# Block sums of the first token group asked for later in a fused window-attention and mixture-of-experts kernel, with its order of issue refitted

## The chip, the cores and the metric

The kernel runs on one core of a Trainium2 chip. The metric is the device time of one launch in microseconds; each version is run several times and the median counts. One more execution is taken with the hardware profiler; every statement about single instructions comes from that one. Five engines run side by side, each with its own queue in program order: PE (matrix products and weight loads), DVE (vector), ACT (scalar: exponentials, copies), POOL (GpSimd) and SP (issue of transfers).

## What is computed

Two layers follow each other. The first is attention over 4 batches, 8 heads, 768 positions and head size 64, in which each position sees the 4 first positions (the sinks) and the last 128. The second is a mixture of 4 experts over the 3072 tokens that come out, each of width 512, with all experts added up under normalised weights:

```python
scores = scale * np.matmul(q, k.transpose(0, 1, 3, 2))
keep = is_sink | in_window
a = np.exp(scores - max); a = a / a.sum(-1)
x = np.matmul(a, v)                  # laid out as (3072, 512)
p = domain_probs / (domain_probs.sum(-1, keepdims=True) + 1e-09)
for e in range(4):
    h = np.maximum(x @ w1[e], 0.0)   # w1[e]: 512 x 1024
    out += p[:, e:e + 1] * (h @ w2[e])
```

## The kernel before

**Tiles and stages.** Each batch of 768 tokens is cut into three groups of 256 tokens, named (batch, group). Attention for a group goes, for each pair of heads, through scores (PE, L704), exponentials (ACT, tile `aT`, L744), a mask (DVE, L752 in batch 0, L725 later), products with the values (PE, tile `od`, L777 and L784), division by the row sum (reciprocal `R` L811 on DVE, then L814 on DVE in batch 0 or L823 on ACT later; result `onat`), and a transposition into `xT`. In batch 0 PE transposes (tile `tx`, L845) and ACT or DVE copies to `xT` (L300); in later batches a transposing DMA does it (L801). Sink scores are separate products (PE, L665), and their exponentials are `sinkA` (ACT, L673). The transposed queries and keys are `qkT`; in batch 0 PE transposes them too (L593, L596) and ACT or DVE copies (L300).

**Experts.** The first layer of an expert is done in one of two ways. The plain way (L1098, tile `hps`) takes eight products of 256 columns per quarter. The fast way is Strassen's scheme: seven half-size products P1, P5, P6, P2, P7, P3, P4 (PE, L1181, tile `cps`) instead of eight. Its moving operands are blocks of `xT` or four sums and differences of them, the **block sums** `T`, formed on DVE by four subtractions (L1150); its weights are blocks of w1 or sums of them (`vf`, or `qkn` for two experts, L402 to L408). Between the products ACT copies partial results (L1224, L1237, L1199), DVE adds (L1231 makes the operand that P7 waits for, L1246 the one that P4 waits for) and applies ReLU and gate (L1215). When a bank of PSUM holds old partial marks, one extra product of 512 columns, the **seed**, clears it (L1189). The second layer is plain for two groups (L1425, tile `acc`, gathered by DVE at L1435 and L1437 into `osb`), and Strassen's scheme for the others (L1350, with sums `S` made on DVE at L1275 and L1296, weight sums `wf` at L367 to L373, results gathered at L1379 to L1397).

**Which units are fast.** `START` says from which (batch, group) on an expert is fast: expert 0 from (1,0), expert 1 from (0,1), experts 2 and 3 from (0,0). So (0,0) needs block sums for experts 2 and 3 and (0,1) for experts 1, 2 and 3.

**What sets the order.** The program is straight-line code; its order is written by a planner that runs while the kernel is built. The planner keeps a clock per engine (`t["pe"]`, `t["dve"]`, ...) from fitted costs. The loop at L1486 lists what PE could do next, each choice with a time from which it is ready and a priority (`LOW_PRODUCT`, `LOW_SECOND`, `EARLY`, `OPEN`, `STEP0` and others, lower first), emits one, and advances the clock. Work for DVE, ACT and POOL is put on a list with a due time (ready time plus a slack such as `GATE`, `GATE0`, `FORM`, `TOKEN0`, `MARGIN`); `flush` (L165) emits it by due time when the planner's clock of that engine reaches it. Work marked "any" goes to ACT or DVE, whichever is free first by that clock: the copies of `tx` and `tr` are such. On the chip each engine then keeps this order and waits on semaphores. The planner's clock is not the chip's.

**Around the change.** `tokens()` (L1130) asks for block sums, one group after another in the order of the groups; at most `NT3` = 3 sets live at a time. A group is asked for when its `xT` is complete by the planner's clock:

```python
at = max(xT_at.get((b, hp, g), 1e12) for hp in range(NHP))
if at > t["pe"]:
    return
```

The four subtractions are then put on DVE's list one after another, each with slack `TOKEN0` in batch 0 (L1149 to L1156). The second reads the result of the first and the fourth that of the second.

Of the kernel before, what the change touches and what calls it, by code (L numbers as in the profile page):

```python
# [16 lines left out]
def kernel(  # L17
# [47 lines left out]
    SHARE_OF = (0.635, 1.148, 0.943)  # L65
    LEAD = (1.227, 0.235)
    DUE = 0
    LOW_PRODUCT = 2.816
    LOW_SECOND = 4.296
    HIGH_PRODUCT = 0.403  # L70
    EARLY = 0.138
    GATE = 5742
    GATE0 = 5043
    FORM = 19230
    FORM2 = 38137
    TOKEN0 = 220
    WAIT2 = 19401
    WAIT1 = 6201
    LATE3 = 3
    TOKEN = 11696  # L80
    MARGIN = 828
    FULL = 8
    STEP0 = 0.155
    READY = 39
    WIDE = 2
    OPEN = 1.336
    ONACT = 1
    ONE = 2
    PAIR = 1
# [16 lines left out]
    t = {"pe": 1200.0, "act": 0.0, "dve": 0.0, "pool": 1280.0, "sp": 800.0, "sw": 6500.0, "hw": 0.0}  # L106
    ring, whole = [0.0] * 6, [False] * 6
    WARM = 6600.0
    FLIP = 179
    LATE = 2342  # L110
    LATE1 = 12449

    def pe(cols, *deps, n=1, switch=0):
# [12 lines left out]
    def dve(cols, *deps, rate=0.96, fixed=157, shared=None):  # L126
        at = max([t["dve"], *deps])
        if rate == 1.92 if shared is None else shared:
            at += max(0.0, port["pool"] - at - 78)
            port["dve"] = at + fixed + cols / rate  # L130
        t["dve"] = at + fixed - 85 + cols / rate
        return at + fixed + 35 + cols / rate
# [10 lines left out]
    def free_at(n=1):  # L143

        return sorted(ring)[n - 1]
# [15 lines left out]
    def later(engine, ready, slack, run):  # L161

        pend.append((ready, ready + slack, engine, run))
# [48 lines left out]
    def sp(*deps, issue=530, takes=600, turning=False):  # L212
        t["sp"] = max([t["sp"], *deps]) + issue
        at = max(t["hw"], t["sp"] + 800)
        row = next((x[3] for x in moved if x[1] <= at < x[2]), 0.0)
        if turning and row:
            t["hw"] = at + TURNED * (row + SHARE)
            t["sw"] += TURNED * SHARE
            for x in moved:
                if x[2] > at:  # L220
                    x[1] += TURNED * SHARE * (x[1] > at)
                    x[2] += TURNED * SHARE
                    landed[x[0]] = x[2] + 900
                    if x[0][0] == "w1" and ("w1", x[0][1]) in landed:
                        landed["w1", x[0][1]] = max(landed["w1", x[0][1]], x[2] + 900)
        else:
            t["hw"] = at + takes + max(0.0, min(takes, t["sw"] - at)) * (not turning)
        return t["hw"] + 900
# [46 lines left out]
    def turn_nat(b, tb):  # L275
# [6 lines left out]
        )  # L282
        turned_at[b, tb] = sp(landed["qk", b, tb], scored_at.get(b - 1, 0.0), issue=1330, takes=1400, turning=True) + (LATE1 if b == 1 else LATE)

# [144 lines left out]
    def next_form():  # L429
# [11 lines left out]
        forming.append(x)  # L441
        later("dve", t["pe"], FORM if x[0] is weight_form1 else FORM2, run)
        return True
# [417 lines left out]
    class Attention:  # L861
# [29 lines left out]
        def options(self):  # L891
# [16 lines left out]
            if self.flips:  # L908
                yield self.flip_ready() + (FLIP if self.b == 0 and self.flips[0][2] else 0), "flip"

# [54 lines left out]
    class Mixture:  # L965
# [77 lines left out]
        def firsts(self):  # L1043
# [4 lines left out]
            for i, u in enumerate(self.open):  # L1048
                b, g, e = u["unit"]
                if u["fast"]:  # L1050
                    for m in u["left"]:
                        yield max(u["at"].get(m, 1e12), free_at() if m == "P5" else 0.0), 2 + STEP0 * i, (u, m)
                else:
                    j = u["left"][0]
                    yield self.unit_ready(b, g, e, j), 2 + STEP0 * i, (u, j)
            if n < WIDE and early:
                at, g = self.next_early()
                yield at, (OPEN if n else 2), ("early", g)
            if n < WIDE and self.units and early <= MIX and self.room() and not (early + zero and self.live >= NH - 1):
                yield self.unit_ready(*self.units[0], QF - 1), (OPEN if n else 2) - EARLY, ("unit",)  # L1060

        def emit_first(self, what, ready):
# [58 lines left out]
            def run(engine):  # L1121
# [5 lines left out]
                part(at)  # L1127
            later("dve", end, GATE0, run)

        def tokens(self):  # L1130

            pairs = [(b, g) for b in range(B) for g in range(NG) if any(self.is_fast(b, g, e) for e in FAST)]
            n = len(self.T)
            if n == len(pairs):
                return
            b, g = pairs[n]
            if n >= NT3 and any((*pairs[n - NT3], e) not in self.finished for e in range(E)):
                return
            at = max(xT_at.get((b, hp, g), 1e12) for hp in range(NHP))
            if at > t["pe"]:  # L1140
                return
            at = t["pe"]
            x = xT[b, g]
            B11, B21, B12, B22 = x[:, 1, 0:2], x[:, 1, 2:4], x[:, 0, 0:2], x[:, 0, 2:4]
            T = sb.tile([P, 4, 2, P], BF16, name="T", tag="T", bufs=NT3)
            self.T[b, g] = {"P1": B11, "P2": B21, "P3": B22, "P4": T[:, 3], "P5": T[:, 0], "P6": T[:, 1], "P7": T[:, 2]}
            steps = [(T[:, 0], B12, B11), (T[:, 1], B22, T[:, 0]), (T[:, 2], B22, B12), (T[:, 3], B21, T[:, 1])]

            def run(engine):  # L1149
                nc.vector.tensor_sub(*steps.pop(0))  # L1150
                done = dve(G, rate=1.92)
                if steps:
                    later("dve", t["dve"], 1500 if b else TOKEN0, run)
                else:
                    self.T_at[b, g] = done
            later("dve", at, TOKEN if b else TOKEN0, run)  # L1156

        def emit_fast(self, u, m, ready):
# [49 lines left out]
            def gated(dst, src, half_, ready, slack, slot=None):  # L1208
                if (b, g) not in PAIRS:
                    plain(dst, src, half_, ready, slack, slot)  # L1210
                    return
                gate = gate_sb[b * NG + g, e][:, half_][:, None, :].to_broadcast([P, QF, P])

                def run(engine):
                    nc.vector.scalar_tensor_tensor(out=dst, in0=src, scalar=0.0, in1=gate, op0=ALU.max, op1=ALU.mult)  # L1215
                    at = dve(n, fixed=152, shared=slot is None)
                    if slot is not None:
                        take(slot, at)
                    part(at)
                later("dve", ready, slack, run)  # L1220
# [21 lines left out]
            elif m == "P2":  # L1242
                gated(H[:, 0, :, 1], y, 1, end, GATE, slots["Y"])
            elif m == "P7":
# [5 lines left out]
            elif m == "P3":  # L1250
                gated(H[:, 0, :, 0], y, 0, end, GATE, slots["V"])
            else:
                gated(H[:, 1, :, 1], y, 1, end, GATE, slots["X"])

# [50 lines left out]
        def until(self, b, g, e, m):  # L1305
            n = self.products.index((b, g, m)) * E + self.order_of(b, g).index(e) - self.piece
            return max(0.0, n * QF * G / 2.4 - MARGIN)

# [177 lines left out]
    while mix.more() or att.more():  # L1486
# [47 lines left out]
        behind = max(t["dve"] - now, 0.0) + 500 * sum(x[2] == "dve" and x[0] < now + 300 for x in pend)  # L1534
        opts.append((max(p + PAD, now), HIGH_PRODUCT if behind > BEHIND or mix.live >= FULL else LOW_PRODUCT, "product", None))
        opts += [(max(f + PAD * (ahead > 0), now), p, "first", x) for f, p, x in mix.firsts()]
        opts.append((max(s2 + PAD * (ahead > 0), now), 1 if mix.since >= 1 else LOW_SECOND, "second", None))
        soonest = min(o[0] for o in opts)
# [58 lines left out]
```

## Time and profile before

| | |
|---|---|
| median of 3 runs | 360.63 us (360.43 to 360.79) |
| the profiled execution | 360.94 us |
| its span, first to last instruction | 359.2 us |
| outside the span in that execution | 1.74 us |
| granted TensorE clock | 1.000 |
| DVE busy | 309.0 us, 703 instructions |
| ACT busy | 168.6 us, 430 instructions |
| POOL busy | 68.9 us, 90 instructions |

A line of a time-ordered view reads: start in us from the begin of the span, duration in us, engine, source line, operation, tiles written and read, shape, how many were merged (x4), and in brackets idle time of the engine just ahead with what ended it. Instructions of one engine overlap in their tails, so the distance between two starts is less than the duration; this distance is what a row of instructions costs. In the view by stretches each engine has its busy time and, in parentheses, its count of instructions.

### The profile page before, as it was taken

The numbers are of one execution on the slowest core, as the hardware profiler recorded it, in microseconds if no ns is written. First come the engines' busy times: TensorE is split into PE (matmuls) and PEld (weight loads), VectorE is DVE, ScalarE is ACT, GpSimd is POOL, SyncE is SP. The second block draws the span as 40 slices with busy tenths as digits, with TensorE's granted clock in tenths as the row PEclk, the third lists the DMA queues.
The fourth block names the chain that finished last, engine by engine and source line by source line (L and its number), as shares of the span: only waits on it lengthen the run. The fifth ranks groups of instructions, "written<-read, shape, count | busy, mean of one in ns | idle before, by whom it ended". The sixth has DMA issues, their size and how long they took to land.

```text
span 359.2 us, 11107 instructions
## 1 busy us (share of the span) xinstructions
PE 349.9 (97%) x4678; PEld 302.7 (84%) x4678; DVE 309.0 (86%) x703; ACT 168.6 (47%) x430; POOL 68.9 (19%) x90
## 2 busy tenths in 40 slices
PE   8899999999999999999999999999999999999995
PEld 3575687777588998998998998899899999999884
DVE  6779889998799799899699799799789899989630
ACT  5856341437883824556444732943752722222110
POOL 8934115211270531020030530000000000000000
PEclk9999999999999999999999999999999999999999
DMA  9999999999994999675077999131042211100011
GB/s 176 186 194 204 222 212 174 145 125 150 202 151 53 151 174 131 75 98 67 31 62 119 151 133 158 47 71 32 20 66 58 59 44 64 31 31 31 1 60 59
DMA packets 115318, 37.86 MB, mean 105 GB/s; under 512 B 97196, under 2 KB 110764, under 8 KB 115268
## 3 DMA queue, kind: packets, MB, share of 16 engines
q0 software_dynamic: 74416, 17.31, 53.3%
q1 hardware_dynamic: 39796, 19.32, 29.9%
q8 instruction: 36, 0.59, 0.7%
q10 hardware_dynamic: 1056, 0.52, 0.6%
q14 instruction: 14, 0.11, 0.1%
HBM read 41.03 MB, written 6.34 MB: 132 GB/s over the span
## 4 chain that ended last, share of the span: by engine, by line
PE 86%; DMA 6%; ACT 3%; DVE 2%; issue 1%; POOL 1%; SPq 0%; ACTq 0%; DVEq 0%
PE cps L1181 38%; PE acc L1350 34%; PE acc L1425 6%; DMA vx<-in_v_dram 3%; PE sps L704 2%; PE od L784 2%; PE hps L1098 2%; DMA kraw<-in_k_dram 2%; DMA scratch<-in_moe_domain_probs_dram 1%; ACT onat L823 1%; ACT aT L744 1%; PE od L777 1%; DVE aT L752 0%; DVE onat L814 0%; DVE osb L1435 0%
## 5 line engine op out<-in xcount | busy, mean ns | idle before, releaser
L1181 PEld LDWEIGHTS <-w 128*128 128x128 bf16 x1408 | 86.3, 98 | 3.2 <-issue 0.8
L1350 PEld LDWEIGHTS <-H 128*128 128x128 bf16 x720 | 66.4, 98 | 8.0 <-issue 1.6
L1215 DVE SCALAR_TENSOR_TENSOR H<-cps,gates 128x512 bf16<-128x512 f32 x105 | 69.6, 684 | 0.0
L1350 PE MATMUL acc<-w,H 128*128 128x256 bf16 x432 | 57.5, 273 | 0.5 <-ACT acc L1379 0.5
L1181 PE MATMUL cps<-T,w 128*128 128x128 bf16 x704 | 52.5, 219 | 0.5 <-DVE cps L1231 0.5
L1181 PE MATMUL cps<-xT,w 128*128 128x128 bf16 x704 | 52.0, 219 | 0.0
L744 ACT ACTIVATE aT<-sps 128x512 bf16<-128x512 f32 (+1 forms) x96 | 46.3, 573 | 3.5 <-PE sps L704 3.4
L1224 ACT COPY cps<-cps 128x512 f32<-128x512 f32 x44 | 25.4, 586 | 46.1 <-PE cps L1181 36.8
L1397 ACT COPY osb<-acc 128x256 f32<-128x256 f32 x40 | 15.2, 379 | 56.9 <-PE acc L1350 49.2
L823 ACT ACTIVATE onat<-od,R 128x64 bf16<-128x64 f32 x144 | 33.1, 352 | 17.8 <-DVE R L811 17.8
L1350 PE MATMUL acc<-wf,H 128*128 128x256 bf16 x288 | 39.2, 273 | 0.0
L1181 PEld LDWEIGHTS <-qkn 128*128 128x128 bf16 x576 | 35.1, 98 | 1.3
L1231 DVE TENSOR_TENSOR cps<-H,cps 128x512 f32<-128x512 f32 x40 | 27.7, 692 | 8.9 <-PE cps L1181 5.3
L1350 PEld LDWEIGHTS <-S 128*128 128x128 bf16 x320 | 30.2, 98 | 4.8 <-issue 1.4
L329 POOL DMA_DIRECT2D vx<-in_v_dram x24 | 21.4, 902 | 62.2 <-PE od L784 50.5
L1237 ACT COPY H<-cps 128x512 f32<-128x512 f32 x40 | 23.4, 593 | 19.3 <-PE cps L1181 19.2
L1425 PE MATMUL acc<-w,H 128*128 128x512 bf16 x128 | 30.1, 379 | 0.0
L1181 PEld LDWEIGHTS <-vf 128*128 128x128 bf16 x480 | 28.6, 98 | 0.3
L1246 DVE TENSOR_TENSOR H<-H,cps 128x512 f32<-128x512 f32 x40 | 27.0, 681 | 0.8 <-PE cps L1181 0.7
L1181 PE MATMUL cps<-T,qkn 128*128 128x128 bf16 x384 | 27.1, 219 | 0.0
L725 DVE TENSOR_TENSOR aT<-aT,mask 128x1024 bf16<-128x1024 bf16 (+1 forms) x36 | 23.1, 641 | 2.4 <-ACT aT L744 2.4
L1215 DVE SCALAR_TENSOR_TENSOR H<-H,gates 128x512 bf16<-128x512 f32 x35 | 23.9, 685 | 0.0
(125 smaller groups left out, 517.9 us busy)
## 6 DMA issues: line engine op xcount, KB each, us to landing
w<-in_moe_w_dram POOLq DMA_DIRECT2D x7, 1024.0 KB, 22.7
out_dram<-osb SPq DMA_DIRECT2D x23, 256.0 KB
gates<-gate_rows SPq DMA_DIRECT2D x40, 128.0 KB
vx<-in_v_dram POOLq DMA_DIRECT2D x24, 128.0 KB, 7.5
rows<-in_q_dram POOLq DMA_DIRECT2D x18, 128.0 KB, 7.0
rows<-in_k_dram POOLq DMA_DIRECT2D x18, 128.0 KB, 7.5
w<-in_moe_w_dram POOLq DMA_DIRECT2D x4, 256.0 KB, 8.8
kraw<-in_k_dram ACTq DMA_DIRECT2D x2, 256.0 KB
```

Of the source, the lines that this page charges most:

```text
L329: nc.gpsimd.dma_start(out=vx[tb][:, :, 0:D], in_=v[b, :, tb * P:(tb + 1) * P, :].rearrange("h p d -> p h d"),)
L725: nc.vector.tensor_mul(x, x, m[:, None, :].to_broadcast([P, n, 2 * w // n]))
L744: nc.scalar.activation(out=a[:, ph], in_=sps[ph][:, 0:w], func=AF.Exp, scale=scale)
L823: nc.scalar.mul(o[:, qi, hp, ph * D:(ph + 1) * D], od[:, qi, ph, 0:D], R[:, qi, ph])
L1181: nc.tensor.matmul(y[:, f], lhsT=A[:, d, f * P:(f + 1) * P], rhs=T[:, d], start=(m in ("P1", "P5") and f == 0 and d == 0), stop=(d == 1), ...
L1215: nc.vector.scalar_tensor_tensor(out=dst, in0=src, scalar=0.0, in1=gate, op0=ALU.max, op1=ALU.mult)
L1224: nc.scalar.copy(out=tiles["Y"], in_=y)
L1231: nc.vector.tensor_add(tiles["V"], c5, tiles["X"])
L1237: nc.scalar.copy(out=c5, in_=y)
L1246: nc.vector.tensor_add(c5, c5, y)
L1350: nc.tensor.matmul(x, lhsT=self.operand(b, g, e, m)[:, f], rhs=forms[e][m][:, f], start=(k == 0 and f == 0 and m in (("P1", "P5", "P2") if ...
L1425: nc.tensor.matmul(op, lhsT=H[:, fb // QF, fb % QF, s], rhs=w2_sb[e][:, fb, :], start=(fb == 0), stop=(fb == NFB - 1),)
```

## The change

One new constant, `TOKEN00`, holds every request for block sums back until the planner's PE clock has passed 35,350 ns. Since requests go in the order of the groups, it moves the sums of (0,0) and, behind them, of (0,1). Slack `TOKEN0` grows from 220 to 699 ns. Thirteen other constants of the planner have new values. No arithmetic is changed, only order.

```diff
-    LOW_PRODUCT = 2.816
-    LOW_SECOND = 4.296
-    HIGH_PRODUCT = 0.403
-    EARLY = 0.138
-    GATE = 5742
-    GATE0 = 5043
-    FORM = 19230
+    LOW_PRODUCT = 2.471
+    LOW_SECOND = 4.227
+    HIGH_PRODUCT = 0
+    EARLY = 0.107
+    GATE = 6210
+    GATE0 = 5056
+    FORM = 20342
     FORM2 = 38137
-    TOKEN0 = 220
+    TOKEN00 = 35350
+    TOKEN0 = 699
...
-    MARGIN = 828
+    MARGIN = 494
...
-    STEP0 = 0.155
-    READY = 39
+    STEP0 = 0.152
+    READY = 35
...
-    OPEN = 1.336
+    OPEN = 1.256
...
-    FLIP = 179
-    LATE = 2342
+    FLIP = 451
+    LATE = 1126
...
-            if at > t["pe"]:
+            if at > t["pe"] or t["pe"] < TOKEN00:
                 return
```

What this does to the five queues, as the two built programs show:

- **DVE.** The four subtractions of (0,0) leave their place between a copy to `qkT` and the first mask of group 1 of attention; the four of (0,1) leave theirs ahead of the reduction at L950. All eight now stand around the last two reciprocal and `onat` pairs of batch 0: two ahead of them, six behind them, and the four of (0,2) follow after the `osb` step of L1435. The last two copies to `xT` of batch 0 leave DVE.
- **ACT** takes those two copies, behind its next ReLU (L1111).
- **PE.** The last two pairs of `tx` transpositions of batch 0 stand behind the next block of eight products of L1425 instead of ahead of it. From there on the order is the same up to the end of attention in batch 1, where one product and the order of P5 and P6 of a unit change places. A longer stretch is regrouped in batch 2, from P2 of unit (2,0) of expert 3 to the product P7 of (2,0), and one seed is no longer needed behind it. Three single swaps follow in (2,2) and (3,0). All other 4677 products are the same.
- **POOL and SP** keep their order; DVE and ACT are regrouped in the same stretches as PE.

## The prediction

> **What bounds the kernel now.** I read the page, then the waits of PE, then the busy time by stretches.
>
> ```profile
> span 359.2 us, 11107 instructions
> PE 349.9 (97%) x4678; PEld 302.7 (84%) x4678; DVE 309.0 (86%) x703; ACT 168.6 (47%) x430; POOL 68.9 (19%) x90
> ```
> ```profile
> PE tx L845 <- DVE onat L814: 1.1, 3, 0.7
> PE acc L1350 <- ACT acc L1379: 0.5, 1, 0.5
> PE cps L1181 <- DVE cps L1231: 0.5, 1, 0.5
> PE sinks L665 <- DVE qkT L300: 0.4, 1, 0.4
> ```
> ```profile
> 38.00:42.00 4.00, 3.74 (x29) 2.35 (x28) 2.84 (x10) 0.66 (x2) 0.00 (x0) 1.00 1.13 223
> 50.30:83.30 33.00, 33.00 (x419) 26.68 (x416) 32.83 (x57) 12.78 (x24) 10.01 (x12) 1.00 1.76 155
> 101.00:230.00 129.00, 128.50 (x1841) 117.25 (x1838) 118.11 (x277) 67.19 (x194) 28.20 (x33) 1.00 1.00 107
> ```
>
> PE is busy for 97% of the span, at full clock (1.00). From 101 to 230 us it idles 0.5 of 129, so there only the number of products counts. What order can win is in the first hundred: the waits above, 2.5 us in all, three of the four rows for DVE. From 50.3 to 83.3 PE and DVE are both full (33.00 and 32.83 of 33), so a gain ahead of that stretch gets through it only if PE and DVE both come to it earlier. Behind it neither is held by more than the listed waits, so what is early at 50 us should stay early to the end.
>
> **Part A: the sums of (0,0) leave 14.23.** DVE, then POOL, PE and ACT around them:
>
> ```profile
> 14.23 0.78 DVE L1150 TENSOR_TENSOR T<-xT 128x256 bf16<-128x256 bf16 x1
> 15.12 0.29 DVE L1150 TENSOR_TENSOR T<-xT,T 128x256 bf16<-128x256 bf16 x1
> 15.33 0.28 DVE L1150 TENSOR_TENSOR T<-xT 128x256 bf16<-128x256 bf16 x1
> 15.74 0.42 DVE L752 TENSOR_TENSOR aT<-aT,mask 128x512 bf16<-128x512 bf16 x1
> 16.07 0.68 DVE L300 COPY qkT<-tr 128x512 bf16<-128x512 bf16 x1
> ```
> ```profile
> 13.81 1.05 POOL L643 TENSOR_TENSOR vsd<-vsf,sel 128x520 bf16<-128x520 f32 x1
> ```
> ```profile
> 16.81 0.27 PE L665 MATMUL sinks<-qkT,ksd 128*32 128x256 bf16 x1 [0.39 <-DVE qkT L300]
> 22.99 0.29 PE L845 MATMUL tx<-ident,onat 128*128 128x128 bf16 x2 [0.66 <-DVE onat L814]
> ```
> ```profile
> 14.67 2.07 ACT L744 ACTIVATE aT<-sps 128x512 bf16<-128x512 f32 x4
> 16.59 0.64 ACT L1111 ACTIVATE H<-hps 128x512 bf16<-128x512 f32 x1
> 17.11 0.39 ACT L673 ACTIVATE sinkA<-sinks 128x256 bf16<-128x256 f32 x1
> 17.50 2.07 ACT L744 ACTIVATE aT<-sps 128x512 bf16<-128x512 f32 x4
> ```
> ```profile
> 18.13 0.43 DVE L752 TENSOR_TENSOR aT<-aT,mask 128x512 bf16<-128x512 bf16 x1 [0.37 <-ACT aT L744]
> 18.64 0.69 DVE L1113 TENSOR_SCALAR H<-hps 128x512 bf16<-128x512 f32 x1
> 22.50 0.42 DVE L814 TENSOR_TENSOR onat<-od,R 128x256 bf16<-128x256 f32 x1
> ```
>
> The four subtractions hold DVE from 14.23 to 15.74, 1.51 us. Without them the mask waits for the first exponential instead. At 17.50 and 18.13 one sees that a mask follows the start of its exponentials by 0.63, so it starts at 14.67 + 0.63 = 15.30, 0.44 earlier. The copy to `qkT` and the sink product of PE that waits for it come 0.44 earlier too. That isn't the gain: ACT runs from 14.67 without a gap (16.59, 17.11, 17.50 stand end to end, starts overlapping tails), its exponentials at 17.50 don't move, and so the mask at 18.13 doesn't. Behind it L1113 at 18.64 waited for PE; with PE 0.44 earlier it is held only by the mask in front, 18.13 + 0.33 (15.74 to 16.07) = 18.46. From there DVE is without a gap to 22.50, so `onat` and the `tx` that waits for it (22.99) come **0.18** earlier; PE waits longer at 22.99 and gives the rest back. Bounds: 0, if L1113 is late for another reason, and 0.44, if ACT lets go earlier. I take 0.18. The sums of (0,1) stand in front of a stretch where DVE waits for PE; taking them away is worth 0.
>
> Here the Trainium skill has a rule that bears on this change. In "SBUF — State Buffer", section "Who interferes with whom", it says that a DVE instruction with two SBUF inputs and a GpSimd instruction that reads SBUF block each other for a whole instruction. The trace agrees: the first subtraction took 0.78 where the others took 0.28 and 0.29, and it lies inside POOL's L643. By this rule the sums would be dear again wherever they land beside such POOL work, which is the third rival; beside an idle POOL it leaves the sum below as it is.
>
> **Part B: the end of attention in batch 0.** PE, then DVE:
>
> ```profile
> 38.47 0.28 PE L845 MATMUL tx<-ident,onat 128*128 128x128 bf16 x2
> 39.02 0.28 PE L845 MATMUL tx<-ident,onat 128*128 128x128 bf16 x2 [0.26 <-DVE onat L814]
> 39.14 1.89 PE L1425 MATMUL acc<-w,H 128*128 128x512 bf16 x8
> 40.87 0.60 PE L1098 MATMUL hps<-xT,w 128*128 128x256 bf16 x4
> ```
> ```profile
> 37.78 0.17 DVE L811 RECIPROCAL R<-od 128x4 f32<-128x4 f32 x1
> 38.88 0.28 DVE L300 COPY xT<-tx 128x256 bf16<-128x256 bf16 x1
> 39.34 0.29 DVE L300 COPY xT<-tx 128x256 bf16<-128x256 bf16 x1 [0.18 <-PE tx L845]
> 41.07 0.75 DVE L1435 TENSOR_SCALAR osb<-acc,scale_t 128x512 f32<-128x512 f32 x1 [0.91 <-PE acc L1425]
> 42.14 0.69 DVE L402 TENSOR_TENSOR vf<-w 128x1024 bf16<-128x1024 bf16 x1
> 47.14 0.75 DVE L1437 SCALAR_TENSOR_TENSOR osb<-acc,scale_t,osb 128x512 f32<-128x512 f32 x1 [0.38 <-PE acc L1425]
> 49.45 0.70 DVE L1231 TENSOR_TENSOR cps<-H,cps 128x512 f32<-128x512 f32 x1 [0.35 <-PE cps L1181]
> ```
>
> PE needs 38.47 to 40.87, 2.40 us, for two pairs of `tx`, a wait for `onat`, and the block of L1425. Now the block comes first: 40.87 − 39.14 = 1.73, then four `tx` at 0.12 a pair (39.02 to 39.14), 0.24. That is 1.97, so **0.43** less; nothing is late in place of the wait, as the second `onat` ends by some 39.4 (37.78 + 0.42 + 1.10 and its tail, worked out below) and `tx` now starts at 40.2.
>
> What the moved sums cost DVE: a subtraction takes 0.21 of its queue (15.12 to 15.33). Two of them ahead of the two reciprocal and `onat` pairs, 0.42, then the pairs, 38.88 − 37.78 = 1.10, then six, 1.26: DVE is free at 37.78 + 2.78 = 40.56. L1435 is wanted 0.20 behind the end of PE's block (41.07 − 40.87), at 38.47 + 1.73 + 0.20 = 40.40, so it starts at 40.56 and is 0.51 earlier than before. The four sums of (0,2) follow it; the copies of `xT` they read now run on ACT, which has 0.66 of work in 38 to 42. L1435 takes about 0.7, four sums some 0.9, and L402 starts near 42.14: where it stood. So the gap of 0.91 and the two copies pay for the eight sums. Behind L402 lie gaps of 0.38 and 0.35, both ended by PE, in which DVE takes up PE's 0.43. Bounds: 0, if DVE isn't free in time and the full stretch starts where it did, and 0.55 (39.02 − 38.47), the whole distance between the two pairs of `tx`. I take 0.43.
>
> Every DMA keeps its place: POOL and SP issue in the old order. The copies moved to ACT make `xT` of (0,2) some 1.5 us later; its first reader is the sum behind L1435.
>
> **Part C: one seed less.**
>
> ```profile
> 231.16 0.38 PE L1189 MATMUL cps<-w 128*128 128x512 bf16 x1
> 231.37 0.61 PE L1181 MATMUL cps<-T,qkn 128*128 128x128 bf16 x8
> ```
>
> It holds PE for 231.37 − 231.16 = **0.21**. PE is the bound there, so this goes to the end.
>
> **The regrouped stretch in batch 2** has the same products and no idle PE. I went through each P7 against the DVE addition (L1231) it waits for, in the new order, with products at their old distances. The tightest place is P7 of unit (2,1) of expert 1:
>
> ```profile
> 216.44 0.69 DVE L1231 TENSOR_TENSOR cps<-H,cps 128x512 f32<-128x512 f32 x1
> 217.03 1.06 PE L1181 MATMUL cps<-T,w 128*128 128x128 bf16 x16
> ```
>
> The addition ends at 217.13 and P7, the second half of the 16, starts near 217.47: 0.34 of room. In the new order one more short DVE step stands ahead, and I put the room at 0.15. Cost 0, bounds 0 and 0.5 (the size of PE's one wait for L1231 in the list of waits). The other swaps of PE, DVE and ACT are of one step each and count 0.
>
> **Sum.** 0.18 + 0.43 + 0.21 = 0.82. The profiled execution took 360.94 (span 359.2 and 1.74 around it), so it would be 360.12; it was 0.31 over the median of the runs, 360.63. Against the median: 360.63 − 0.82 = 359.81.
>
> **Rivals.**
>
> 1. *The full stretch swallows it.* If DVE doesn't reach the stretch at 50 us earlier, PE waits longer behind it, and of A and B nothing is left: 360.63 − 0.21 = 360.4. For it: DVE is full for 33 us, and the new sums leave it at 42.14 where it was. Against it: the gaps at 47.14 and 49.45, 0.73 together, wait for PE. Chance 0.17; with a stall of 0.5 in the regrouped stretch it is 360.9.
> 2. *More than I count.* All of 0.44 in A and 0.55 in B: 360.63 − 0.44 − 0.55 − 0.21 = 359.4. For it: DVE and PE are both 0.44 ahead at 16 us. Against it: ACT has no gap from 14.67 to the exponentials at 17.50. Chance 0.13.
> 3. *Slower: the moved sums are blocked.* A blocked subtraction cost 0.78 − 0.28 = 0.5 more. DVE has 0.18 + 0.91 + 0.38 + 0.35 = 1.82 of gaps from 39 to 49.5, and the copies gone are worth 0.57; the eight sums at 0.285 need 2.28. That leaves 0.11 to spare, so from the first blocked sum on B's gain is eaten up and then DVE comes late to its full stretch, which goes to the end. With three blocked: 1.5 − 0.11 − 0.18 − 0.21 = 1.00 slower, 361.6; it is slower than before from where 0.5 a sum exceeds 0.50 in all, that is from the second on. Against it: POOL has 0.00 busy from 38 to 42. Chance 0.13 for this size or beyond.
> 4. *It doesn't do what it says.* The built order shows the sums moved, so no chance is set aside.
>
> **How the numbers follow.** The forecast has 0.57. A measurement of this kernel can tell about 0.2%, 0.72 us, from no change, that is, times under 359.91. The forecast lies just beyond it; of its 0.57 I count 0.40 as faster and 0.17 as within. Rival 2 is faster, rival 1 within, rival 3 slower. Faster 0.53, same 0.34, slower 0.13. The range goes from 359.2, a little under rival 2, to 361.0, a little over rival 1 with its stall; it leaves out rival 3 and a little on each side.
>
> **What would show it.** In the new profile: no subtraction before 37 us; PE's wait for sinks near 0, its wait at the second `tx` near 23 us longer, about 0.9; no wait of `tx` near 39 us; the products of L1098 behind the block near 40.3 instead of 40.87; all eight sums at 0.28 to 0.29; the full stretch of DVE starting near 48.8 instead of 49.45; one seed fewer. I would be wrong if PE's wait for L1231 behind 83 us grows by what was won, if any moved sum takes 0.78, or if new waits stand between 206 and 225 us.

## The result and the profile after

| | before | changed |
|---|---|---|
| median and range, 9 runs each on one chip | 360.63 us (360.43 to 361.19) | 359.70 us (359.44 to 360.90) |
| ratio, 95% interval | | 0.9978 (0.9969 to 0.9987) |
| on a second chip run, 20 and 8 runs | 360.74 us | 359.78 us, ratio 0.9972 (0.9963 to 0.9982) |
| the profiled execution | 360.94 us, span 359.2 | 359.44 us, span 357.7 |

The changed kernel is 0.93 us faster (360.63 − 359.70), 0.96 in the second measurement; the forecast was 0.82. The interval excludes a change of zero, but it reaches from 0.47 to 1.12 us, so the times alone can't tell 0.82 from 0.92; for the parts the traces have to be read. The profiled executions differ by 1.50, which is more than the medians do; where the rest comes from is shown below (0.44 of it is an accident of the first profiled execution of the kernel before, and 0.08 was there before the first instruction that the change moves). In the changed kernel's file every line number from 76 on is one higher: L1150 is L1151, L1425 is L1426, L1201 is L1202. The same holds for E1 to E4 and for E6 to E10.

The page of the changed kernel, and the waits of PE (microseconds in all, times, longest):

```profile
span 357.7 us, 11089 instructions
PE 348.9 (98%) x4668; PEld 302.7 (85%) x4677; DVE 306.8 (86%) x701; ACT 169.1 (47%) x432; POOL 69.0 (19%) x90
```
```profile
PE tx L846 <- DVE onat L815: 0.8, 2, 0.7
PE acc L1351 <- ACT acc L1380: 0.5, 1, 0.5
```

Against the list of before, the wait for sinks (0.4) is gone, the wait of `tx` near 39 us (0.26 of the 1.1) is gone, and so is the wait of 0.5 for the addition that P7 needs. To see where each bit was won, I matched the PE instructions of two traces and took the median difference of their starts in stretches of 10 us. Each column below is a kernel against the first trace of before; negative is earlier. E1 to E4 and E9 are experiments that follow.

| stretch from, us | changed | E1 late sums only | E2 regrouping only | E3 first sums only | E4 `tx` behind the block only | E9 before again |
|---|---|---|---|---|---|---|
| 10 | −0.08 | −0.02 | 0.04 | −0.06 | 0.08 | 0.01 |
| 20 | −0.35 | −0.29 | 0.04 | −0.34 | 0.31 | 0.04 |
| 30 | −0.44 | −0.37 | 0.14 | −0.42 | 0.23 | 0.08 |
| 40 | −0.89 | −0.83 | 0.14 | −0.42 | −0.23 | 0.08 |
| 70 | −0.89 | −0.83 | 0.14 | −0.42 | −0.23 | 0.07 |
| 90 | −1.33 | −0.84 | 0.08 | −0.85 | −0.66 | −0.37 |
| 200 | −1.38 | −0.54 | 0.28 | −0.89 | −0.70 | −0.42 |
| 230 | −1.60 | −0.54 | 0.06 | −0.52 | −0.70 | −0.42 |
| 350 | −1.49 | −0.55 | 0.19 | −0.51 | −0.70 | −0.45 |

The steps of the changed kernel are: 0.27 to the stretch from 20 and 0.09 more to that from 30 (part A), 0.45 to that from 40 (part B), nothing lost through the full stretch of DVE, 0.44 at 84 us, 0.22 at 231 (part C), and 0.11 given back by 291. The 0.08 of the first row is no step: this execution simply began that much earlier.

**Part A in the trace after.** DVE, then ACT, then PE, at the place where the sums of (0,0) stood:

```profile
15.23 0.43 DVE L753 TENSOR_TENSOR aT<-aT,mask 128x512 bf16<-128x512 bf16 x1 [0.99 <-ACT aT L745]
...
17.95 0.43 DVE L753 TENSOR_TENSOR aT<-aT,mask 128x512 bf16<-128x512 bf16 x1 [0.70 <-ACT aT L745]
...
22.15 0.42 DVE L815 TENSOR_TENSOR onat<-od,R 128x256 bf16<-128x256 f32 x1
```
```profile
16.51 0.65 ACT L1112 ACTIVATE H<-hps 128x512 bf16<-128x512 f32 x1
16.98 0.45 ACT L674 ACTIVATE sinkA<-sinks 128x256 bf16<-128x256 f32 x1
17.25 2.14 ACT L745 ACTIVATE aT<-sps 128x512 bf16<-128x512 f32 x4
```
```profile
16.05 0.52 PE L666 MATMUL sinks<-qkT,ksd 128*32 128x256 bf16 x4
...
22.63 0.29 PE L846 MATMUL tx<-ident,onat 128*128 128x128 bf16 x2 [0.66 <-DVE onat L815]
```

The mask starts at 15.23, as predicted (15.30, less the 0.08 by which this execution began earlier). ACT's second set of exponentials starts at 17.25 instead of 17.50, which the prediction had ruled out; 0.08 of this is the earlier beginning, 0.17 is not. The distances say why. From L1112 to `sinkA` it is now 16.98 − 16.51 = 0.47, before it was 17.11 − 16.59 = 0.52, and PE's sink product of before ended at 16.81 + 0.27 = 17.08, just ahead of 17.11. From `sinkA` to the exponentials it is now 17.25 − 16.98 = 0.27, before it was 17.50 − 17.11 = 0.39, and the scores that they read were made right behind that sink product (from 17.01). So ACT had waited twice, 0.05 and 0.12, too short to be listed.

All five traces of this case that have the sums at 14 us show it: `sinkA` starts 0.30 or 0.31 behind the start of that product, also where the product came later (17.12 and 17.43 in E4), and the exponentials 0.38 or 0.39 behind `sinkA`; in the seven traces without the sums there it is 0.26 or 0.27. That the second wait is for the scores is read from the order of PE. Behind it everything moved: `onat` from 22.50 to 22.15, `tx` from 22.99 to 22.63, with the same wait of 0.66.

**Part B in the trace after.** PE, then DVE:

```profile
38.02 1.89 PE L1426 MATMUL acc<-w,H 128*128 128x512 bf16 x8
39.75 0.39 PE L846 MATMUL tx<-ident,onat 128*128 128x128 bf16 x4
39.98 1.25 PE L1099 MATMUL hps<-xT,w 128*128 128x256 bf16 x10
```
```profile
37.34 0.49 DVE L1151 TENSOR_TENSOR T<-xT 128x256 bf16<-128x256 bf16 x2
37.74 0.18 DVE L812 RECIPROCAL R<-od 128x4 f32<-128x4 f32 x1
...
39.65 0.49 DVE L1151 TENSOR_TENSOR T<-xT,T 128x256 bf16<-128x256 bf16 x2
40.05 0.75 DVE L1436 TENSOR_SCALAR osb<-acc,scale_t 128x512 f32<-128x512 f32 x1
...
41.71 0.69 DVE L403 TENSOR_TENSOR vf<-w 128x1024 bf16<-128x1024 bf16 x1
...
48.55 0.69 DVE L1232 TENSOR_TENSOR cps<-H,cps 128x512 f32<-128x512 f32 x1 [0.35 <-PE cps L1182]
```

From the block of products to L1099 it is 39.98 − 38.02 = 1.96, where the working had 1.97. Two merged sums take 0.48 to 0.49 and the next instruction starts 0.40 behind the pair, so none was blocked. The gap of 0.35 ahead of L1232 is as long as before, and the whole row stands 0.90 earlier (49.45 − 48.55): the full stretch took the gain over.

### The profile page after: what moved, and what is told of

It reads as the page before. It is cut to its first block, busy times and chain, and to the rows that moved or that the text cites. A ratio compares the mean times of both kernels' runs of the same rounds, so it can differ in the third digit from the quotient of the medians.

```text
span 357.7 us, 11089 instructions
## 1 busy us (share of the span) xinstructions
PE 348.9 (98%) x4668; PEld 302.7 (85%) x4677; DVE 306.8 (86%) x701; ACT 169.1 (47%) x432; POOL 69.0 (19%) x90
## 4 chain that ended last, share of the span: by engine, by line
PE 87%; POOL 4%; DMA 3%; ACT 3%; DVE 1%; issue 1%; POOLq 0%; DVEq 0%
PE cps L1182 38%; PE acc L1351 34%; PE acc L1426 6%; DMA vx<-in_v_dram 3%; PE sps L705 3%; PE od L785 2%; PE hps L1099 2%; ACT onat L824 1%; POOL vx L330 1%; POOL qkn L260 1%; POOL w L343 1%; PE od L778 1%; ACT aT L745 1%; ACT H L1200 0%; PE sinks L666 0%
## 5 line engine op out<-in xcount | busy, mean ns | idle before, releaser
L1232 DVE TENSOR_TENSOR cps<-H,cps 128x512 f32<-128x512 f32 x40 | 27.8, 694 | 8.8 <-PE cps L1182 5.1
L1426 PE MATMUL acc<-w,H 128*128 128x512 bf16 x119 | 29.0, 379 | 0.6 <-issue 0.2
```

Of the source, the lines that this page charges most:

```text
L1232: nc.vector.tensor_add(tiles["V"], c5, tiles["X"])
L1426: nc.tensor.matmul(op, lhsT=H[:, fb // QF, fb % QF, s], rhs=w2_sb[e][:, fb, :], start=(fb == 0), stop=(fb == NFB - 1),)
```

## The experiments

My theory: the gain is A + B + C, each from the wait that the prediction names; the other swaps of the regrouping are worth nothing. Rival: the gain is made by the regrouping that the refitted constants bring, and the late sums alone would end in new waits. Expectations use the line numbers of the changed kernel where they name one of its lines.

**E1, the late sums alone.**

```diff
+    TOKEN00 = 35350
...
-            if at > t["pe"]:
+            if at > t["pe"] or t["pe"] < TOKEN00:
```


> The kernel before with nothing but the late sums: those of the first token group are held back until the second group is in the experts, every other constant and so every regrouping and all seeds as before. My theory: parts A and B come from the place of the sums alone and the new order's other swaps are worth nothing, so it is A and B without C, 0.3 to 0.4 and 0.43 to 0.45 off: 359.8 to 359.9 us, with the products of L1099 behind the block starting near 40.0 and the full stretch of DVE near 48.6. Rival: the regrouping of the other constants makes the gain and the late sums alone end in new waits: 360.4 to 360.7.

Measured: 360.00 against 360.85, ratio 0.9972 (0.9961 to 0.9983). PE in this kernel:

```profile
38.09 1.89 PE L1426 MATMUL acc<-w,H 128*128 128x512 bf16 x8
...
40.04 2.13 PE L1099 MATMUL hps<-xT,w 128*128 128x256 bf16 x18
...
87.72 0.34 PE L1182 MATMUL cps<-xT,qkn 128*128 128x128 bf16 x3 [0.26 <-issue]
```

The rows at 38 and 40 us are those of the changed kernel to 0.07 us, and the ratio is as good. The rival is excluded by the interval. No other constant is changed here, so the gate alone also puts `tx` behind the block. The column of E1 seems to gain nothing at 84 us; in fact it gains the 0.44 there and loses 0.42 in the third row, in the middle of a product, for no reason that the profile shows. (Other single traces lose a few tenths too, each at a place of its own: this one another 0.30 near 195 us, E2 0.23 near 134, E3 0.37 near 221. This wasn't pursued.)

**E2, the regrouping alone.**

```diff
-    TOKEN00 = 35350
+    TOKEN00 = 0
```


> The changed kernel with the sums of the first token group let go at once, as before: the regrouping and the missing seed stay. My theory: only C is left, 0.21 off: 360.4 us, and PE stands at 40.87 behind the block as in the kernel before. Rival (the regrouping makes the gain): 359.7 to 359.9.

Measured: 360.94 against 360.85, ratio 1.0000 (0.9991 to 1.0009). PE's wait for `onat` is back:

```profile
38.61 0.29 PE L846 MATMUL tx<-ident,onat 128*128 128x128 bf16 x2
39.16 0.29 PE L846 MATMUL tx<-ident,onat 128*128 128x128 bf16 x2 [0.26 <-DVE onat L815]
...
41.01 1.25 PE L1099 MATMUL hps<-xT,w 128*128 128x256 bf16 x10
```

The rival falls: without the late sums nothing is gained that these runs can see. The 0.21 of C is inside the interval (0.9994) and not shown by the times. The trace shows both what C is and what it lost. The step of 0.22 where the seed stood is there (from 0.28 to 0.06 between the stretches from 200 and 230), and by 291 us 0.12 is given back, as in the changed kernel. DVE of the changed kernel, where that begins, and of before:

```profile
269.13 0.28 DVE L1151 TENSOR_TENSOR T<-xT 128x256 bf16<-128x256 bf16 x1
269.44 0.29 DVE L1151 TENSOR_TENSOR T<-xT,T 128x256 bf16<-128x256 bf16 x1
```
```profile
273.33 0.29 DVE L1150 TENSOR_TENSOR T<-xT,T 128x256 bf16<-128x256 bf16 x1
273.53 0.29 DVE L1150 TENSOR_TENSOR T<-xT 128x256 bf16<-128x256 bf16 x1
```

In the new order a sum stands directly behind the one whose result it reads, and starts 0.31 behind it (269.44 − 269.13). In the old order the first sum of this set stood at 271.93, other work came between, and the ones left follow at 0.20 (273.33 to 273.53). The difference of 0.11 is what DVE loses, and as DVE has no gap from there, PE has lost it too by 291.10, where P5 and P6 of a unit start. All five traces in the new order lose 0.10 to 0.13 there against the first trace of before, the six others in the old order nothing. That this pair is the cause is read from the rows; it wasn't undone by itself.

**E3, part A alone.**

```diff
+    TOKEN00 = 22000
...
-            if at > t["pe"]:
+            if at > t["pe"] or t["pe"] < TOKEN00:
```


> The kernel before with the first eight sums moved only from 14.23 us to about 23 us; all orders of PE, ACT, POOL and SP as before, so this is part A alone. My prediction's working gives 0.18: 360.45. The trace of the changed kernel suggests 0.29 to 0.37, because ACT's sink exponential at 17.11 had waited for PE's sink product: 360.3. Rival: what DVE saves at 14 us it pays again at 23 us, where it has no gap of 0.5: 360.6 or more.

(In fact the four sums of (0,0) move; those of (0,1) stand near there already.) Measured: 360.56 against 360.85, ratio 0.9991 (0.9983 to 1.0000). The sums in their new place:

```profile
22.51 0.28 DVE L1151 TENSOR_TENSOR T<-xT 128x256 bf16<-128x256 bf16 x1
22.83 0.29 DVE L1151 TENSOR_TENSOR T<-xT,T 128x256 bf16<-128x256 bf16 x1
```

PE gains 0.28 by the stretch from 20 and 0.36 by that from 30. The second step is another small wait of before that goes, for a copy to `qkT`:

```profile
31.23 0.40 PE L704 MATMUL sps<-qkT 64*128 64x128 bf16 x6 [0.19 <-DVE qkT L300]
```

DVE was late with that copy since 27 us, through another meeting with GpSimd. GpSimd and DVE of before, then DVE of E3:

```profile
26.63 0.75 POOL L342 DMA_DIRECT2D w<-in_moe_w_dram  x1 [0.22 <-issue]
```
```profile
27.10 0.26 DVE L951 TENSOR_SCALAR rs<-rs 128x24 f32<-128x24 f32 x1
```
```profile
26.77 0.18 DVE L952 TENSOR_SCALAR rs<-rs 128x24 f32<-128x24 f32 x1
```

The same small instruction takes 0.26 in the first trace of before, 0.31 in E9 and 0.36 in E2, each time ending 0.02 ahead of the end of GpSimd's issue (27.36 against 27.38 in the first); it takes 0.18 in the nine others. So 0.08 of A hangs on the moment at which a transfer is issued.

So A is 0.36, not 0.18; the time's interval (0 to 0.6) holds both, and the traces decide. The rival is not borne out: DVE has room at 23 us.

**E4, part B alone.**

```diff
-... for r, step in att.options()]
+... for r, step in att.options() if not (step == "turn" and att.valued[0][1:] == (2, 2) and mix.second and mix.second[0] == (1, 1, 0))]
```


> The kernel before with the sums where they were (14.23 us) and only the two last pairs of tx of batch 0 moved behind the block of products of L1426; so part B alone. My theory: PE's wait for onat near 39 us goes, 0.43 off: 360.2, L1099 behind the block near 40.4. Rival: without the eight sums in that place DVE meets the block differently or the full stretch of DVE from 50 us on swallows it: 360.6.

Measured: 360.40 against 360.85, ratio 0.9991 (0.9983 to 1.0000); the interval (0 to 0.6) holds the 0.43 but reaches to nothing, so here too the trace decides. (In the built order the last two copies to `xT` go to ACT as well, as they do in the changed kernel.) DVE, and PE behind the block:

```profile
40.62 0.75 DVE L1436 TENSOR_SCALAR osb<-acc,scale_t 128x512 f32<-128x512 f32 x1 [1.43 <-PE acc L1426]
```
```profile
38.69 1.89 PE L1426 MATMUL acc<-w,H 128*128 128x512 bf16 x8
40.42 0.39 PE L846 MATMUL tx<-ident,onat 128*128 128x128 bf16 x4
40.64 1.58 PE L1099 MATMUL hps<-xT,w 128*128 128x256 bf16 x13
```

PE goes from 0.23 behind to 0.23 ahead, 0.46 in all, and keeps it. The gap of 1.43 on DVE is the room into which the change lays its sums: eight of them at 0.20 a piece would take 1.6, and with them (E1) B is 0.46 all the same. So B needs the new place of `tx`, not the sums; the sums fill a gap that it opens.

This trace starts B from a debt, and the row that made it is worth a look. Its first sum, left at 14 us, beside GpSimd's L644:

```profile
14.31 1.02 DVE L1151 TENSOR_TENSOR T<-xT 128x256 bf16<-128x256 bf16 x1
```

It took 1.02 where before took 0.78, and PE is 0.31 late at 20 us. In the five traces with this place it took 0.78, 0.79, 0.82, 0.92 and 1.02, and ended 0.15 to 0.17 behind the end of GpSimd's instruction every time: the end of that one sets its length, and the first trace of before paid least. Part A takes this spread away along with the mean.

**E5, the ReLU at 84 us.** The changed kernel's trace gains 0.44 there, which no step of the prediction names. GpSimd and DVE of before:

```profile
83.80 0.88 POOL L269 DMA_DIRECT2D rows<-in_k_dram  x1
```
```profile
84.05 0.88 DVE L1201 TENSOR_SCALAR H<-H 128x512 bf16<-128x512 f32 x1
84.85 0.68 DVE L1231 TENSOR_TENSOR cps<-H,cps 128x512 f32<-128x512 f32 x1
```

The same ReLU takes 0.43 in the changed kernel. Here it starts 0.25 behind GpSimd's issue, ends 0.25 behind the end of it (84.93 against 84.68), and the addition behind it is the one for which PE waits 0.50. The Trainium skill has a rule for such a pair: in "SBUF — State Buffer", section "Who interferes with whom", a `tensor_scalar` on DVE can enter a mode that takes the port pair shared with GpSimd, and whichever instruction comes first keeps it to its end. The rows agree that the two hold each other up (0.88 against 0.43); which of them came first can't be read off the recorded starts, as E9 shows.

```diff
-    LOW_PRODUCT = 2.816
+    nth = []; LOW_PRODUCT = 2.816
...
-                    if engine == "act":
+                    if engine == "act" or nth.append(0) or len(nth) == 2:
                         nc.scalar.activation(out=dst, in_=src, func=AF.Relu)
```


> The kernel before with one instruction moved: the ReLU of DVE that starts at 84.05 us there and takes 0.88 us runs on ACT; nothing else differs. My theory: it took 0.88 instead of 0.43 because GpSimd's issue of the row load at 83.80 had begun before it, PE's wait of 0.50 for L1231 at 85.58 is the price, and the kernel before pays it in most of its executions. Without the ReLU there PE's wait is gone and the time is 0.4 lower, near 360.4. Rivals: the collision is rare and the profiled execution an odd one: 360.8 in the median; or PE is held by something else next and the wait comes back under another name: 360.8.

Measured: 360.64 against 360.57, ratio 0.9997 (0.9988 to 1.0006). In the trace PE's wait is gone and PE is 0.38 ahead from there on; the median isn't. My theory's 0.4 lies at the very end of the interval (360.57 × 0.9988 = 360.14), so it isn't quite excluded; the medians fit its first rival better, that few executions of the kernel before pay this. E9 shows one that doesn't; how many do isn't shown.

**E6, ten seeds.**

```diff
-            if m == "P1" and unset:
+            if m == "P1" and (unset or b == 2):
...
-                pe(QF * P)
+                if unset: pe(QF * P)
```


> The changed kernel with ten seeds more, all in batch 2, in places that need none (what they write is written over); the order of everything else is unchanged. My theory: PE is the bound there and each seed costs its 0.21, 2.1 in all over the changed kernel, 361.7 to 361.9. Rival: a part of them falls into time in which PE would have waited for DVE, which is just as full in batch 2, and costs nothing: half, 360.7 to 360.9.

Measured: 361.73 against 360.57, ratio 1.0032 (1.0019 to 1.0045). Against the changed kernel's 0.9972 to 0.9978 that is 0.0054 to 0.0060, 1.95 to 2.16 us for ten. In the trace PE is 1.54 later at the end than at 70 us, where the changed kernel is 0.60 earlier: 2.14. A seed costs its 0.21 each time; the rival falls. So C is a real 0.21, and 0.11 of it was lost by the pair of sums above.

**E7, the third rival made to happen.**

```diff
-    LOW_PRODUCT = 2.471
+    LOW_PRODUCT = 2.471; summed = []
...
+            [nc.gpsimd.tensor_add(beside, y[:, i], y[:, i]) for y in summed for i in range(2)]; summed.clear()
             nc.gpsimd.dma_start(
                 out=vx[tb][:, :, 0:D],
...
-    vsf = consts.tile([P, B, DX], FP32, name="vsf")
+    vsf = consts.tile([P, B, DX], FP32, name="vsf"); beside = consts.tile([P, P], BF16, name="beside")
...
-                nc.vector.tensor_sub(*steps.pop(0))
+                y = steps.pop(0); nc.vector.tensor_sub(*y); summed.append(y[0]) if b == 0 and g < 2 else None
```


> The changed kernel with GpSimd made busy beside the moved sums: after each of the eight sums GpSimd adds the first operand of it to itself, in two additions of 128x128, into a tile that nobody reads. This is the third rival of the prediction made to happen. If GpSimd's additions block the sums: the sums between 38.8 and 40 us take up to 0.3 longer each (an addition of 128x128 should take a quarter of the 1.05 of 128x520), the full stretch of DVE begins later and the time is 0.5 to 1.7 above the changed kernel, 360.2 to 361.4. If DVE goes first and GpSimd waits: the sums stay at 0.28 to 0.29 and the time is that of the changed kernel, 359.7.

(The additions read the result of each sum, and in GpSimd's queue they stand ahead of the next load of v, so they run as long as GpSimd takes for all 16, past the sums.) Measured: 360.17 against 360.57, ratio 0.9992 (0.9984 to 1.0001), which is 0.5 to 0.7 us above the changed kernel's ratios. Its DVE, and GpSimd's additions by group (count, duration in ns as least, median, most):

```profile
39.32 0.68 DVE L1151 TENSOR_TENSOR T<-xT 128x256 bf16<-128x256 bf16 x2
39.92 0.69 DVE L1151 TENSOR_TENSOR T<-xT,T 128x256 bf16<-128x256 bf16 x2
...
45.52 0.88 DVE L368 TENSOR_TENSOR wf<-w 128x1024 bf16<-128x1024 bf16 x1
...
49.47 0.68 DVE L1232 TENSOR_TENSOR cps<-H,cps 128x512 f32<-128x512 f32 x1
```
```profile
L330 POOL TENSOR_TENSOR beside<-T x16: 394/528/929, 37.7 to 47.2; 128x128 bf16<-128x128 bf16 x16
```

Of each pair shown one sum takes 0.48 and the other 0.28 as before: of the eight, three are held, by 0.08, 0.20 and 0.20. A weight sum behind them takes 0.88 instead of the 0.68 of the same one in the changed kernel; the additions (0.39 at the least, 0.53 in the median) pay as well. DVE comes to its full stretch without the gap and 0.92 later than in the changed kernel (49.47 − 48.55), and PE's lead over the first trace of before falls from 0.91 to 0.31.

So the mechanism of the third rival is real, and what gets past the gaps goes to the end as it said. Its size was not 0.5 a sum: 0.5 was the price beside one GpSimd instruction of 1.05, beside these short ones it is 0.20 at the most. And most of the price here isn't that of the eight sums. They delay DVE by 0.48 (to 40.53), those of (0,2) by 0.31 more and the weight sums by another 0.56, 1.35 in all at 46.32; of this the gaps up to 50 us take all but 0.62. By these figures they would have taken the 0.48 of the eight alone; that wasn't run.

**E8, late but elsewhere.** As E3, with `TOKEN00 = 30000`.

> The kernel before with the first eight sums moved to another late moment: between the copy of qkT at 30.49 and the masks at 31.69 us, where DVE has no gap. Orders of PE, ACT, GpSimd and SP as before. My theory: being late is not what helps, the place is; here eight sums at 0.21 hold the masks back by about 1.5, the products of L785 that wait for them begin 1.0 to 1.5 later, and with A's 0.3 off the time is 361.4 to 362. Rival: anything behind 14 us serves, since the masks have room: 360.4.

Measured: 360.52 against 360.57, ratio 1.0000 (0.9991 to 1.0009). ACT, DVE, PE, and PE's wait for `onat`:

```profile
29.67 1.56 ACT L301 COPY qkT<-tr 128x512 bf16<-128x512 bf16 x3
```
```profile
32.20 0.28 DVE L1151 TENSOR_TENSOR T<-xT,T 128x256 bf16<-128x256 bf16 x1
32.41 1.09 DVE L753 TENSOR_TENSOR aT<-aT,mask 128x512 bf16<-128x512 bf16 x3
...
34.07 0.75 DVE L753 TENSOR_TENSOR aT<-aT,mask 128x512 bf16<-128x512 bf16 x2
```
```profile
33.97 0.22 PE L778 MATMUL od<-vsd,sinkA 128*128 128x130 bf16 x1
...
34.14 0.22 PE L778 MATMUL od<-vsd,sinkA 128*128 128x130 bf16 x1
...
34.62 0.22 PE L778 MATMUL od<-vsd,sinkA 128*128 128x130 bf16 x1
```
```profile
PE tx L846 <- DVE onat L815: 0.8, 2, 0.7
```

The order of ACT isn't quite as before: the planner gave it the second copy to `qkT` of this place (three instead of two), which spares DVE about 0.6. My theory falls here by its size. The first mask is 0.7 later than before (32.41 against 31.69) and not 1.5, for a good part because of that copy and of A's lead, and the products that read them come by PE's order only at 33.78, so that PE loses 0.3 at one of them (34.14 to 34.62, 0.48, where the set before took 0.17), not 1.0 to 1.5. Half of that comes back: PE now comes later to `tx` near 39 us, and the wait there is gone from the list (two waits, as in the changed kernel, not three). PE is 0.28 ahead of the first trace of before from 40 us on, where E3 is 0.42. The rival's 360.4 lies inside the interval (360.57 × 0.9991 = 360.25 at its lower end). So in the traces the place matters, by 0.14 at the end and 0.3 on the way, and it is not what makes A; with the copy on DVE it might have cost more, which wasn't run.

**E9 and E10, both kernels again.**

> The kernel before, unchanged, for a second trace of it. If the collision of the ReLU at 84 us with GpSimd's issue is what most of its executions pay, it stands in this trace too: the ReLU at 0.8 to 0.9 and PE's wait for L1232 near 85.6. If it is an accident of the first profiled execution, the ReLU takes 0.43, there is no such wait, and this profiled execution is about 0.4 shorter than the first one's 360.94: near 360.5.

> The changed kernel, unchanged, beside the kernel before on one chip, for a second ratio and a second trace. By the sum A 0.36, B 0.45, C 0.11 net, 0.92 in all, the ratio is 0.9974, and the new trace against that of the kernel before shows PE 0.36, then 0.81, then 0.92 ahead, with or without another 0.44 from the collision at 84 us. If the prediction's smaller A (0.18) were right, the ratio is 0.9980 and the trace shows 0.18 at 20 us.

Measured: E9's profiled execution took 360.49, its runs 360.84 in the median against 360.74 for the same program's other runs (ratio 1.0008, 1.0000 to 1.0017: so much do two sets of runs differ). E10: 359.78 against 360.74, ratio 0.9972 (0.9963 to 0.9982). GpSimd and DVE in E9:

```profile
83.97 1.05 POOL L270 DMA_DIRECT2D rows<-in_k_dram  x1
```
```profile
84.12 0.43 DVE L1202 TENSOR_SCALAR H<-H 128x512 bf16<-128x512 f32 x1
```

GpSimd's issue starts 0.17 later than in the first trace. Now the ReLU, 0.15 behind it, goes first and takes 0.43, and the issue pays, 1.05 instead of 0.88. PE has no wait there. So the collision was an accident of the first profiled execution of before, and of the 1.50 between the two profiled executions 0.44 belongs to it. E10's trace ends 1.54 ahead of the first one of before and E9's 0.45, so the second pair differs by 1.09. Of this 0.28 is there before the first moved instruction. From then on E10 is ahead of E9 by another 0.32 in the stretch from 20 and 0.13 in that from 30 (A is 0.45 here, as E9's first sum took 0.82 and its L952 0.31), 0.45 in that from 40 (B), loses 0.18 at 87 us as E1 did, and then has 0.21 and −0.12 (C): 0.81 in all, against the 0.92 expected: 0.09 more in A, and the loss of 0.18. The ratio's interval holds 0.9974 as well as 0.9980; that A isn't 0.18 is shown by the traces.

## Why the prediction was right

The time was right (359.81 forecast, 359.70 and 359.78 measured), the direction too, and the change is clear of the noise (the interval ends at 0.9987). By its steps:

- **Part B, 0.43: right.** 0.45 in the changed kernel, 0.46 alone (E4) and 0.46 with the sums but without the regrouping (E1). The distance from the block to L1099 (1.97) came out at 1.96. L403 stands 0.43 earlier (42.14 to 41.71), which is A's 0.36 and the earlier beginning and no more: next to it the eight sums cost DVE nothing, as worked out.
- **Part A, 0.18: the place right, the size wrong.** It is 0.36. The step that failed is "ACT runs from 14.67 without a gap …, its exponentials at 17.50 don't move": they moved by 0.17 beyond the earlier beginning. Two of the ends that had been read as back to back were waits, of 0.05 and 0.12, for PE's sink product and what stands behind it, and that product itself stood behind the sums. Of the 0.17 the next mask took up 0.10 (18.13 to 17.95, less 0.08), and this adds to the 0.18 (0.27 by `onat`, less the 0.08). A further 0.08 came from the wait at 31.23, which was not looked at, and hangs on an issue of GpSimd's. The bound of 0.44 held it.
- **Part C, 0.21: right for the seed** (0.22 in the traces of the changed kernel and of E2, 0.21 each in E6), **wrong for what lay beside it.** "The other swaps … count 0" missed 0.11, the pair of dependent sums at 269.13. C nets 0.1.
- **The regrouped stretch, 0: right.** No wait for L1232 stands in the list of the changed kernel.
- **The sum.** 0.36 + 0.45 + 0.22 − 0.11 = 0.92, against 0.93 and 0.96 in the medians. That these agree to some hundredths is luck: two sets of runs of one program differ by more (E9). That 0.82 came so near is in part two errors of opposite sign, +0.18 in A and −0.11 in C.
- **The profiled execution and the median.** Putting the sum against the median as well was worth it: the profiled execution of before held an accident of 0.44, which the changed kernel's doesn't have, and the traces alone would have given 1.5.
- **The rivals.** The first (the full stretch swallows A and B) is out: all rows from 40 to 84 us carry the same lead. The second (more than I count) was half right, A nearly full, B not. The third didn't happen, since GpSimd was idle; E7 shows its mechanism, at less than half its size. Its margin of 0.11 was also too narrow: it counts a sum as 0.285, its duration, where part B counts the distance of 0.21. With that the margin is 1.82 + 0.57 − 8 × 0.21 = 0.71, in E7 the gaps took 0.73, and in the changed kernel the gap of 0.35 ahead of L1232 was still there with all eight sums in. Where the prediction has the first subtraction inside L643, it begins inside it and ends 0.15 behind it (15.01 against 14.86).
- **What would show it.** Seen as listed: no subtraction before 37 us, no wait for sinks, none of `tx` near 39, sums at 0.28 to 0.29, one seed fewer, no new wait from 206 to 225. Not as listed: the wait at the second `tx` is 0.66 and not 0.9, L1099 stands at 39.98 and not 40.3, the full stretch of DVE at 48.55 and not 48.8. The last two are A's missing 0.18, with the 0.08 by which this execution began earlier. The wait is no longer than before because `onat` came 0.27 earlier and not 0.18, and PE 0.28 and not 0.44 (its products behind the scores from 17.56 to 17.20).

What stays open: how often the kernel before pays the collision at 84 us (in one of its two traces; also 0.82 for that ReLU in E2's), the few tenths that E1, E2, E3 and E10 lose at places of their own, and whether the pair of sums at 269 us is what costs C its 0.11.

## What to carry to other kernels

Four subtractions whose results PE first read at 47.8 us held, at 14 us, a copy, a product, an exponential and through them PE. Moving them was worth 0.2 to 0.4 at each of the three places tried (23, 30 and 37 us), because the place that they left was the dear one. A wait of PE at the end of a stage goes when work that is ready is put ahead of it (E4: 0.46), and the gap that this opens on the other engine is a place for the work that was moved. When instructions of an engine seem to stand end to end, compare the distances with the same pair elsewhere before calling it bound, and before taking a trace's wait for a cost, look whether the median or a second trace has it.

## What the hardware showed unexpectedly

- A `tensor_scalar` of DVE from 128x512 f32 to bf16 takes 0.43, and 0.88 or 0.82 when GpSimd's issue of a software transfer has begun 0.25 or 0.28 before it (E2), 0.55 when it has begun 0.56 before (E7); begun 0.10 to 0.16 before it (E4, E9, E8), the ReLU keeps 0.43 and the issue takes 1.00 to 1.06 instead of 0.88. One tenth of a microsecond in the start of a transfer decides over 0.44 on PE. A small one (128x24, 0.18) is held in the same way, up to 0.36 (E2).
- A DVE subtraction of 128x256 starts 0.20 behind one that it doesn't depend on and 0.31 behind one whose result it reads.
- A subtraction with both inputs in SBUF that meets a GpSimd instruction of 1.05 ends 0.15 to 0.17 behind the end of that one, in all five traces, so it pays 0.5 to 0.7 (0.78 to 1.02 against 0.28); beside additions of 0.39 to 0.93 it pays up to 0.20 (E7).
